# Lightning attention with a SwiGLU feed-forward block: the statements after the first chunks in a new, written-out order

## The chip, the cores and the metric

The kernel runs on one core of a Trainium2 chip. The metric is the device time of one execution in microseconds (us), as the median of several runs; less is better. The core has five engines that matter here, each with its own queue, which it works through in order: TensorE (PE in the profile; its weight loads are PEld), VectorE (DVE), ScalarE (ACT), GpSimd (POOL) and SyncE (SP), which only issues DMAs. They wait for each other through semaphores. Matmul results go to PSUM, which the kernel uses as eight banks of 128 partitions by 512 float32 columns.

## The reference

The input is q, k and v of shape 4 x 8 x 768 x 64 (batch, heads, positions, head size), a decay `lam` per head, and three weight matrices. The attention is linear, with a decay, in blocks of 64 positions:

```python
for b in range(nb):
    intra = einsum('bhic,bhjc->bhij', qb, kb) * Dmask      # inside the block
    intra = einsum('bhij,bhjd->bhid', intra, vb)
    inter = einsum('bhid,bhde->bhie', qb * lam_pow, kv_state)   # all earlier blocks
    out[:, :, sl] = intra + inter
    kv_state = lam_block * kv_state + einsum('bhsd,bhse->bhde', kb * rev_pow, vb)
```

Its result, as 3072 tokens of 512 values, goes through the feed-forward block, with 1536 hidden columns:

```python
g, val = x @ w_gate, x @ w_val
return (g * sigmoid(g) * val) @ w_out
```

## The kernel before, in words

**Attention.** The work is cut into 12 groups, numbered 0 to 11, of one pair of batches' 128 positions each (all eight heads). For each group the kernel loads q, k and v as float32, casts k and q to bf16 with the decay factors (`cast_scaled`: k on ScalarE, L291, q on VectorE or GpSimd, L293), transposes them by a DMA on SyncE's queue (L279), and scales v (`v_scale`, L266, mostly GpSimd). Then TensorE does four things in 64x64 tiles: `upd_mm` (L424, the sum of k times v that updates the state), `scores` (L362 or, from group 6 on, L392), `inter` (L518, queries times state) and `intra` (L531, masked scores times v). Most have 32 small matmuls. Around them, ScalarE copies the update out of PSUM (`upd_copy`, L438 and L446), GpSimd adds it to the running state (`state`, L459 to L483), VectorE multiplies the scores by the causal mask (L369, L397), and ScalarE's `guard` (L502) copies one column of the result between `inter` and `intra`, which share two banks, so that the second doesn't write into a bank while the first is still on its way. Last, `evac` (L544, L547) copies the result into `xt`, the input of the feed-forward block.

**Feed-forward.** Two groups make a tile of 512 tokens; there are six tiles, 0 to 5. In tiles 0 to 3 the hidden columns are taken in 12 chunks of 128: `ffn_gate` has four matmuls (L585), and ScalarE's silu of the result (L590); `ffn_val` has four (L603), and VectorE's multiplication with that silu (L607) gives the hidden values h. Tile 1 and the first chunks of tile 2 work on halves of 256 tokens, so there the matmuls have 256 columns instead of 512. Tile 0's output is a plain product (L623). Tiles 1 to 5 get their output by a Strassen-like scheme of seven products instead of eight (`out_units`, L823; p1 to p7), and tiles 4 and 5 use the same scheme for gate and value too (`ffn_unit`, L733, in three units per tile, with bank sums on VectorE at L775 and L783, copies on ScalarE at L767 and L770, and one of four multiplications on GpSimd, L763). The scheme needs sums of its operands: of the hidden values (`h_combo`, L670), of the weights (`w_combo`, L696, and `wo_combo`, L653) and of the inputs (`x_combo`, L714). All of these are on VectorE.

**What sets the order.** The first stretch, up to tile 0's chunk 1, is written out statement by statement. Behind it a plan decides: `steps` lists the feed-forward chunks, `at` hangs an attention part, a load or a sum behind a chunk, and a loop works through the chunks and hands out waiting work on the way: masks through `later`, sums through `trickle` (`drip` gives out one or two per chunk), state copies through `kvq`. Banks are taken in turn, 0 to 7 and around again, by `bank()`, where the plan doesn't set another start. From tile 2's output on, statements are written out, still with `drip` in between. A group's four TensorE parts stand mostly together, as in `attend`, called for groups 6 to 9:

```python
core_a(g)               # inter, guard
upd_mm(g + 1); upd_copy(g + 1)
scores(g + 1)
core_b(g)               # masks, intra, evac
state(g + 1)
```

Each engine runs its own instructions in the order in which the statements put them in its queue. Tile pools hand out buffers: four for the silu results, for instance, so that a chunk's silu waits until the multiplication four chunks earlier is done.

Of the kernel before, what the change touches and what calls it, by code (L numbers as in the profile page):

```python
# [37 lines left out]
def _body(ctx, tc, nc, q, k, v, lam, moe_w_gate, moe_w_val, moe_w_out, out):  # L38
# [13 lines left out]

    NAT0 = 6
    NB = 4
# [212 lines left out]
    def load_group(g, parts="kqv"):  # L271
        for src, what in ((k, "kraw"), (q, "qraw"), (v, "v")):
            if what[0] in parts:
                load_fp32(g, nc.scalar if what == "kraw" and g in KACT else nc.sync, src, what)

    def dma_transpose(g):
        t = st[("qk", g)]
        tt = qkt_pool.tile([128, 2, 2, HP, 128], BF16, name="qkt", tag="qkt")
        nc.sync.dma_start(out=tt.rearrange("p a s h n -> p (a s h) n"),  # L279
                          in_=t.rearrange("p a s x -> p (a s x)"), transpose=True)  # L280
        st[("qkt", g)] = tt
        for put in held.pop(g, []):
            put()

    QP = ()

    def cast_scaled(g, eng=nc.vector):
        eng = nc.gpsimd if g in QP else eng
        t = qk_pool.tile([128, 2, 2, H * D], BF16, name="qk", tag="qk")
        st[("qk", g)] = t  # L290
        nc.scalar.copy(out=t[:, 0].rearrange("p s (h d) -> p h s d", h=H),  # L291
                       in_=st[("kraw", g)].rearrange("p h (s d) -> p h s d", s=2))
        eng.tensor_tensor(out=t[:, 1].rearrange("p s (h d) -> p h s d", h=H),  # L293
                                in0=st[("qraw", g)].rearrange("p h (s d) -> p h s d", s=2),
                                in1=qfac(g), op=ALU.mult)
        dma_transpose(g)
# [38 lines left out]
    KACT = ()  # L335
    HOLD = {(1, 1): 10}
    held = {}
# [6 lines left out]
    def scores(g, cs=(0, 1), warm=0):  # L344
# [9 lines left out]
        for c in cs:  # L354
# [12 lines left out]
            for h2 in range(2):  # L367
                def do_mask(c=c, h2=h2):
                    nc.vector.tensor_tensor(  # L369
                        out=ssb[:, h2, 2 * c:2 * c + 2].rearrange("p a s n -> p a (s n)"),  # L370
                        in0=sp[(c, h2)].rearrange("p (a x) -> p a x", a=2),
                        in1=bap(causal, [[0, 2], [1, 2 * BLK]]),
                        op=ALU.mult)
                later.append(do_mask)
# [5 lines left out]
    def scores_n(g):  # L380
# [14 lines left out]
        for h2 in range(2):  # L395
            def do_mask(h2=h2):
                nc.vector.tensor_tensor(out=ssb[:, h2], in0=sp[h2].rearrange("p (a x) -> p a x", x=M),  # L397
                                        in1=bap(causaln, [[0, 2 * HP], [1, M]]), op=ALU.mult)
            later.append(do_mask)

    def upd(g):
        upd_mm(g)
        upd_copy(g)
        state(g)
# [58 lines left out]
    def kv_flush(age=0, m=9):  # L463
        while kvq and m and len(kvq_now) - kvq[0][0] >= age:
            kvq.pop(0)[1]()
            m -= 1

    def state(g):
# [5 lines left out]
        for n, u in enumerate(us):  # L474
# [9 lines left out]
            elif len(kv) == n + 1:  # L484
                o = kv_pool.tile([128, HP, D], BF16, name="kvn", tag=f"kvn{n}", bufs=2)
                kv.append(o)
                if g in KVA:
                    kvq.append((len(kvq_now), lambda g=g, n=n, o=o, f=f: kv_copy(g, n, o, f, nc.scalar.copy)))
                else:
                    kv_copy(g, n, o, f, nc.gpsimd.tensor_copy)  # L490


# [45 lines left out]
    def evac(g, fns=(nc.scalar.copy, nc.scalar.copy)):  # L538
        op, xt = st[("op", g)], st[("xt", g // 2)]
        for r in range(2):  # L540
            if fns[r] is None:
                continue
            if g < NAT0:
                fns[r](out=xt[:, g % 2, :, r].rearrange("p h (m s) -> p h s m", s=2),  # L544
                       in_=op[r].rearrange("p (h s m) -> p h s m", h=HP, s=2))
            else:
                fns[r](out=bap(xt, [[BLK, 2 * MC], [1, 2], [2, M // 2]], g % 2 * MC * 2 * BLK + r * M),  # L547
                       in_=op[r].rearrange("p (b e x) -> p b e x", b=2 * HP, e=2))
# [12 lines left out]

    def core(g, fns=(nc.scalar.copy, nc.scalar.copy)):
        core_a(g)
        core_b(g, fns)

# [65 lines left out]
    def take(n, seeded, cols):  # L631


        got = [(ring[0] + i) % 8 for i in range(n)]
        ring[0] += n
        yes = [x for x in got if primed[x] >= cols][:len(seeded)]
        assert len(yes) == len(seeded)
        rest = [x for x in got if x not in yes]
        return [yes.pop(0) if i in seeded else rest.pop(0) for i in range(n)]

# [14 lines left out]
    def h_combo(t, j, g=None):  # L655


        fs = slice(0, FH) if g is not None else slice(2 * j[0], 2 * j[1]) if type(j) is tuple else slice(2 * j, 2 * j + 2)
        g0, g1 = (0, B // 2) if g is None else (g, g + 1)
# [3 lines left out]
        for i in range(3):  # L663
            if ("hs", t, i) not in st:
                st[("hs", t, i)] = raw_pool.tile([128, FH, B // 2, BLK], BF16, name="hs", tag="raw")
# [624 lines left out]
```

## Time and profile before

| | |
|---|---|
| time, median of 3 runs | 217.0 us (216.41 to 217.78) |
| span of the profiled execution | 215.0 us (no other time of its own is given) |
| granted TensorE clock | 1.000 of full speed |
| TensorE matmul | 208.1 us busy, 97% |
| TensorE weight load | 153.3 us, 71% |
| VectorE | 148.3 us, 69% |
| ScalarE | 130.9 us, 61% |
| GpSimd | 92.7 us, 43% |
| moved by DMA | 39.76 MB |

The span goes from the first to the last instruction that the profiler records on the core. Busy time is the sum of an engine's instructions. A line of the timeline gives the start in us, the length in us, the engine, the program's line, the operation, out<-in by the program's names, and how many instructions are joined; what stands in brackets is the idle time ahead of it and what ended that. Matmuls overlap in their pipeline, so the length of a matmul line is longer than the time to the next one; distances between starts are the better measure. In a group line, the two numbers behind the bar are the busy time in us and the mean of one in ns; then follows the engine's idle time just before them and what ended it.

### The profile page before, as it was taken

The numbers are of one execution on the slowest core, as the hardware profiler recorded it, in microseconds if no ns is written. First come the engines' busy times: TensorE is split into PE (matmuls) and PEld (weight loads), VectorE is DVE, ScalarE is ACT, GpSimd is POOL, SyncE is SP. The second block draws the span as 40 slices with busy tenths as digits, with TensorE's granted clock in tenths as the row PEclk, the third lists the DMA queues.
The fourth block names the chain that finished last, engine by engine and source line by source line (L and its number), as shares of the span: only waits on it lengthen the run. The fifth ranks groups of instructions, "written<-read, shape, count | busy, mean of one in ns | idle before, by whom it ended". The sixth has DMA issues, their size and how long they took to land.

```text
span 215.0 us, 6856 instructions
## 1 busy us (share of the span) xinstructions
PE 208.1 (97%) x2797; PEld 153.3 (71%) x2801; DVE 148.3 (69%) x267; ACT 130.9 (61%) x280; POOL 92.7 (43%) x128
## 2 busy tenths in 40 slices
PE   8789999999999999999999999999999999999993
PEld 3467445887888548866754545888888888888883
DVE  1773447576677989874569878697988389961940
ACT  5878676756636153638369487774983676636522
POOL 6675755818399440595962153240750022200200
PEclk9999999999999999999999999999999999999999
DMA  6999999999999778899576859855000500005014
GB/s 188 345 354 381 376 336 296 285 226 223 309 387 174 185 212 208 244 214 263 122 198 143 217 121 257 207 121 201 5 3 5 195 0 3 0 0 198 0 52 146
DMA packets 82176, 39.76 MB, mean 185 GB/s; under 512 B 45410, under 2 KB 77794, under 8 KB 82146
## 3 DMA queue, kind: packets, MB, share of 16 engines
q1 hardware_dynamic: 80946, 38.74, 64.7%
q10 hardware_dynamic: 1200, 0.59, 0.9%
q8 instruction: 22, 0.36, 0.7%
q14 instruction: 8, 0.07, 0.1%
HBM read 28.31 MB, written 6.29 MB: 161 GB/s over the span
## 4 chain that ended last, share of the span: by engine, by line
PE 93%; DMA 2%; DVE 1%; SPq 1%; ACT 0%; issue 0%; DVEq 0%
PE bank L823 22%; PE bank L585 20%; PE bank L603 19%; PE bank L733 17%; PE bank L623 5%; PE bank L531 3%; DMA kraw<-in_k_dram 2%; PE bank L518 2%; PE bank L424 2%; PE bank L362 1%; DVE ssb L369 1%; SPq L115 1%; PE bank L392 1%; PE bank L322 1%; ACT qk L306 0%
## 5 line engine op out<-in xcount | busy, mean ns | idle before, releaser
L607 DVE TENSOR_TENSOR h<-sil,bank 128x256 bf16<-128x256 bf16 (+1 forms) x67 | 35.0, 533 | 29.9 <-PE bank L603 17.2
L585 PE MATMUL bank<-xt,wg_sb 128*128 128x256 bf16 (+1 forms) x276 | 52.8, 315 | 0.0
L603 PE MATMUL bank<-xt,wv_sb 128*128 128x256 bf16 (+1 forms) x276 | 52.5, 314 | 0.0
L590 ACT ACTIVATE sil<-bank 128x256 bf16<-128x256 f32 (+1 forms) x67 | 31.6, 481 | 21.8 <-PE bank L585 18.4
L603 PEld LDWEIGHTS <-wv_sb 128*128 128x128 bf16 x276 | 26.9, 98 | 14.8 <-POOL wv_sb L249 0.2
L585 PEld LDWEIGHTS <-wg_sb 128*128 128x128 bf16 x276 | 25.9, 98 | 13.6 <-issue 0.2
L266 POOL TENSOR_TENSOR v_s<-v,dec 128x512 bf16<-128x512 f32 (+1 forms) x18 | 23.0, 1295 | 24.3 <-DMA v<-in_v_dram 17.3
L763 POOL TENSOR_TENSOR h<-sil,es 128x512 bf16<-128x512 bf16 x6 | 7.0, 1165 | 47.4 <-ACT sil L760 47.4
L823 PEld LDWEIGHTS <-h 128*128 128x128 bf16 x240 | 23.3, 98 | 3.4 <-issue 0.3
L823 PE MATMUL bank<-wo_sb,h 128*128 128x256 bf16 x180 | 21.5, 273 | 0.0
L823 PEld LDWEIGHTS <-hs 128*128 128x128 bf16 x180 | 17.6, 98 | 2.7
L369 DVE TENSOR_TENSOR ssb<-bank,causal 128x512 bf16<-128x512 f32 x24 | 15.4, 684 | 1.8 <-PE bank L362 1.8
L479 POOL TENSOR_TENSOR kvf<-kvs,ups 128x256 f32<-128x256 f32 x8 | 6.5, 814 | 20.9 <-ACT ups L446 20.9
L733 PEld LDWEIGHTS <-ws 128*128 128x128 bf16 x144 | 13.8, 98 | 1.8
L823 PE MATMUL bank<-wt,hs 128*128 128x256 bf16 x120 | 15.0, 273 | 0.0
L775 DVE TENSOR_TENSOR bank<-bank,es 128x512 f32<-128x512 f32 x12 | 7.8, 694 | 9.6 <-PE bank L733 9.6
L479 POOL TENSOR_TENSOR kvf<-kvf,ups 128x256 f32<-128x256 f32 x16 | 13.0, 815 | 0.9
L760 ACT ACTIVATE sil<-bank 128x512 bf16<-128x512 f32 x18 | 10.5, 596 | 3.7 <-PE bank L733 3.7
L733 PE MATMUL bank<-xs,ws 128*128 128x256 bf16 x96 | 12.6, 273 | 0.0
L763 DVE TENSOR_TENSOR h<-sil,bank 128x512 bf16<-128x512 bf16 x18 | 11.8, 683 | 0.3 <-ACT sil L760 0.3
L623 PE MATMUL bank<-wo_sb,h 128*128 128x512 bf16 x45 | 10.7, 380 | 0.2
L733 PE MATMUL bank<-xt,wg_sb 128*128 128x256 bf16 x72 | 10.8, 273 | 0.0
(119 smaller groups left out, 360.3 us busy)
## 6 DMA issues: line engine op xcount, KB each, us to landing
out_dram<-osb SPq DMA_DIRECT2D x22, 256.0 KB, 2.6
v<-in_v_dram SPq DMA_DIRECT2D x18, 256.0 KB, 4.6
woraw<-in_moe_w_out_dram SPq DMA_DIRECT2D x6, 512.0 KB, 7.1
kraw<-in_k_dram SPq DMA_DIRECT2D x24, 128.0 KB, 3.4
qraw<-in_q_dram SPq DMA_DIRECT2D x24, 128.0 KB, 3.4
wraw<-in_moe_w_gate_dram SPq DMA_DIRECT2D x5, 512.0 KB, 6.9
wraw<-in_moe_w_val_dram SPq DMA_DIRECT2D x5, 512.0 KB, 7.0
kraw<-in_k_dram SPq DMA_DIRECT2D x4, 512.0 KB, 6.3
```

The source lines that it names most:

```text
L266: eng.tensor_tensor(out=st[("vs", g)][:, h0:h1], in0=st[("v", g)][:, h0:h1].rearrange("p h (s d) -> p h s d", s=2), in1=vfac(g, h0, h1), o ...
L369: nc.vector.tensor_tensor(out=ssb[:, h2, 2 * c:2 * c + 2].rearrange("p a s n -> p a (s n)"), in0=sp[(c, h2)].rearrange("p (a x) -> p a x", ...
L479: nc.gpsimd.tensor_tensor(out=o, in0=f, in1=u, op=ALU.add)
L585: nc.tensor.matmul(gp[:, n0:n1], wg_sb[:, mc, fs], xt[:, g0:g1, mc].rearrange("p g b n -> p g (b n)"), start=(mc == 0 and n0 == 0), stop=( ...
L590: nc.scalar.activation(sil[:, 0:N], gp[:, 0:N], AF.Silu)
L603: nc.tensor.matmul(vp[:, n0:n1], wv_sb[:, mc, fs], xt[:, g0:g1, mc].rearrange("p g b n -> p g (b n)"), start=(mc == 0 and n0 == 0), stop=( ...
L607: nc.vector.tensor_tensor(out=h_sb[:, fc % FH, b0:b1].rearrange("p b n -> p (b n)"), in0=sil[:, 0:N], in1=vp[:, 0:N], op=ALU.mult)
L623: nc.tensor.matmul(ps, st[("h", t, fc // FH)][:, fc % FH, b], wo_sb[:, fc, c0:c1], start=(fc == 0), stop=(fc == FC - 1))
L733: nc.tensor.matmul(o[:, fi * 256:fi * 256 + 256], lhs(i, c, 2 * j + fi), rhs(c), start=(start and fi == 0 and c == 0), stop=(c == KH - 1), ...
L760: nc.scalar.activation(sil[key], src, AF.Silu)
L763: eng.tensor_tensor(out=h_of(half, r), in0=v3(sil[half, r]), in1=v3(src), op=ALU.mult)
L823: nc.tensor.matmul(o, lhs(f), rhs(f), start=(start and f == 0), stop=(f == FH - 1), skip_group_check=True)
```

## The change

Everything up to tile 0's chunk 1 stays. From tile 0's third chunk on, the plan, the loop that works through it and the queues of waiting work are gone, and all statements are written out one by one, in another order. The functions are cut into smaller pieces for that: `core_a` and `core_b` become `op_new`, `inter`, `guard`, `intra` and `evr`; `cast_scaled` becomes `kcast` and `qcast`; `ffn_unit` becomes `unit`, `uprod` (one product with its copy or sum), `silu` and `mu`; `out_units` becomes `out_new`, `oprod` and `store`; `h_combo` becomes `hsum`, one sum each. `use(...)` names the banks for the statement behind it. `hsum`, `x_combo` and `w_combo` take the engine as an argument.

The computation, its tiles and its 2797 matmuls are the same. What moves: some chunks, or their value halves, now stand between the parts of a group's attention (groups 2, 3, 4 and 9, and group 10 in tile 4's second unit); gate and value chunks come in pairs in places; the q casts of groups 4 and 9, one weight sum (in three pieces), two input sums and seven sums of h go from VectorE to GpSimd; k cast 4 and some result copies go from ScalarE to VectorE; half the v scalings of groups 8 and 11 go from GpSimd to VectorE; the last output tile takes its products in another order.

```diff
-    def cast_scaled(g, eng=nc.vector):
-        eng = nc.gpsimd if g in QP else eng
...
+    def kcast(g, fn=nc.scalar.copy):
+        fn(out=qk_new(g)[:, 0].rearrange("p s (h d) -> p h s d", h=H),
+           in_=st[("kraw", g)].rearrange("p h (s d) -> p h s d", s=2))
+
+    def qcast(g, eng=nc.vector):
+        eng.tensor_tensor(out=qk_new(g)[:, 1].rearrange("p s (h d) -> p h s d", h=H),
...
+    def evr(g, r, fn):
         op, xt = st[("op", g)], st[("xt", g // 2)]
...
-    def core_a(g):
-        kv_flush()
+    def op_new(g):
         st[("op", g)] = [bank() for _ in range(2)]
         covered(2 * HP * D, 2)
-        inter(g, True)
-        guard(g)
-
-    def core_b(g, fns=(nc.scalar.copy, nc.scalar.copy)):
-        run_later(len(later))
-        intra(g, False)
-        evac(g, fns)
...
+    def hsum(t, k, f0, f1, g0=0, g1=2, eng=None):
+        fs = slice(f0, f1)
...
+        (eng or nc.vector).tensor_tensor(out=o, in0=i0, in1=i1, op=op)
+
+    def pair(o, i0, i1, op, eng=None, parts=1):
+        n = o.shape[-1] // parts if len(o.shape) == 3 else 0
...
-    at(s0["11a"], upd_core, 2, SPLIT)
-    at(s1a[7], scores, 3)
-    at(s1a[7], upd_mm, 3)
-    at(s1a[10], core_upd, 3, SPLIT, (0, 1))
-    at(s1b[9], core_upd, 4, SPLIT)
...
+    use(2, 3); upd_mm(2)
+    use(4, 5); op_bare(2)
+    intra(2, True)
+    guard(2)
+    upd_copy(2, (0,))
+    use(0); ffn_gate(0, 11, 0, 2)
+    inter(2, False)
+    evr(2, 0, DVEC)
+    evr(2, 1, ACTC)
...
+    kcast(4, DVEC)
+    use(3); ffn_val(1, 1, 0, 2)
+    state(2)
+    qcast(4, nc.gpsimd)
...
+    use(0, 4, 2, 3); scores(3)
+    use(6); ffn_gate(1, 8, 0, 2)
+    use(1, 5); upd_mm(3)
+    use(7); ffn_gate(1, 9, 0, 2)
+    upd_copy(3)
+    state(3)
+    use(6, 5); op_new(3)
...
+    use(3); ffn_val(1, 9, 0, 2)
+    use(7); ffn_val(1, 8, 0, 2)
+    mask(3, 1, 0)
+    inter(3, True)
+    guard(3)
+    use(3); ffn_gate(1, 10, 0, 2)
+    use(0, 1); upd_mm(4)
+    intra(3, False)
...
+    inter(4, True)
+    guard(4)
+    use(3); ffn_val(1, 9, 2, 4)
+    intra(4, False)
+    use(6, 7); upd_mm(5)
+    evr(4, 0, DVEC)
+    evr(4, 1, DVEC)
...
+    use(4, 5); op_new(7)
+    inter(7, True)
+    use(6, 7); upd_mm(8)
+    guard(7)
+    upd_copy(8)
+    intra(7, False)
+    use(0, 1); scores(8)
...
+    inter(9, True)
+    use(2, 3); upd_mm(10)
+    guard(9)
+    upd_copy(10)
+    use(4, 5); scores(10)
+    use(6); ffn_gate(3, 11, 0, 4)
+    intra(9, False)
+    evr(9, 0, ACTC)
+    evr(9, 1, ACTC)
+    hsum(2, 2, 4, 6, 0, 2, nc.gpsimd)
...
+    use(2, 4); upd_mm(11)
+    upd_copy(11)
+    state(11)
+    unit(4, 1, (3, 5, 2, 4, 6, 7))
+    uprod(4, 1, 0, 0)
+    uprod(4, 1, 0, 1)
+    intra(10, False)
...
+    mu(4, 1, 1, 1, nc.gpsimd)
+    uprod(4, 1, 5, 1)
+    uprod(4, 1, 5, 0)
```

More of the change, by code (lines that the diff above doesn't have):

```diff
@@ L395, in scores_n @@
         for h2 in range(2):
[L396 to L404, printed above, removed]
+            st[("sp", g, 0, h2)] = sp[h2]
+            later.append(lambda h2=h2: mask(g, 0, h2))
     def upd_mm(g, up=None):
@@ L755, in v3, with mu @@
+    def mu(t, j, half, r, eng=nc.vector):
         def v3(x):
             return x.rearrange("p (f g n) -> p f g n", f=2, g=2)
[L758 to L767 removed]
@@ new lines, in _body @@
+    use(7); ffn_val(2, 1, 0, 2)
+    use(0); ffn_gate(2, 2, 0, 2)
+    use(1); ffn_val(2, 2, 0, 2)
+    w_combo(1, 0, (0, 3), nc.gpsimd)
+    wo_combo(1)
+    use(2); ffn_gate(2, 3, 0, 2)
+    use(3); ffn_val(2, 3, 0, 2)
+    use(4); ffn_out(0, 0)
+    use(5, 1); op_new(5)
+    inter(5, True)
+    guard(5)
+    use(7, 0, 6, 2); scores(5)
+    mask(5, 0, 0)
+    mask(5, 1, 0)
+    mask(5, 0, 1)
+    mask(5, 1, 1)
+    use(3); ffn_out(0, 1)
+    intra(5, False)
+    kcast(6)
+    evr(5, 1, ACTC)
@@ new lines, in _body @@
+    use(5); ffn_val(3, 2, 0, 4)
+    use(3); ffn_val(3, 7, 0, 4)
+    hsum(2, 3, 0, 4, 0, 2)
+    hsum(2, 0, 4, 6, 0, 2)
+    use(6); ffn_gate(3, 3, 0, 4)
+    use(7); ffn_val(3, 3, 0, 4)
+    use(0, 1); op_new(8)
+    inter(8, True)
+    guard(8)
+    use(2, 3); upd_mm(9)
+    upd_copy(9)
+    use(4, 5); scores(9)
+    intra(8, False)
+    evr(8, 0, DVEC)
+    evr(8, 1, ACTC)
+    state(9)
+    use(6); ffn_gate(3, 8, 0, 4)
+    use(7); ffn_val(3, 8, 0, 4)
+    mask(9, 0, 1)
+    kcast(10)
+    qcast(10, nc.vector)
```

1144 lines of the change are left out of this document (709 added, 435 removed).

## The prediction

> **What bounds the kernel now.** I read the summary of the page first, then its chain, then TensorE's timeline from 15 us on.
>
> ```profile
> PE 208.1 (97%) x2797; PEld 153.3 (71%) x2801; DVE 148.3 (69%) x267; ACT 130.9 (61%) x280; POOL 92.7 (43%) x128
> ...
> PE 93%; DMA 2%; DVE 1%; SPq 1%; ACT 0%; issue 0%; DVEq 0%
> ...
> L763 POOL TENSOR_TENSOR h<-sil,es 128x512 bf16<-128x512 bf16 x6 | 7.0, 1165 | 47.4 <-ACT sil L760 47.4
> ```
>
> TensorE is busy 208.1 of 215.0 us and is 93% of the chain. Of its 6.9 us of idle time, 3.3 lie behind its last matmul (211.69, the last copies and stores, unchanged) and about 2.5 before 15 us (unchanged). So VectorE, ScalarE and GpSimd set the end only where a short wait of TensorE is theirs. The granted clock is 1.000 throughout, and the streaming rate doesn't move: a full-width matmul of 512 columns takes 0.216 us, one of 256 columns 0.109. The change keeps all 2797 matmuls with their shapes, so only two things can move the end: waits of TensorE, and what it loses between full-width work and the attention's 64x64 tiles (a **visit** below).
>
> Waits first, from TensorE's timeline:
>
> ```profile
> 37.51 0.45 PE L424 MATMUL bank<-v_s,qk 64*64 64x64 bf16 x32
> 37.79 0.67 PE L531 MATMUL bank<-ssb,v_s 64*64 64x128 bf16 x32
> 38.73 0.41 PE L518 MATMUL bank<-qkt,kvn 64*64 64x128 bf16 x8 [0.28 <-ACT guard L502]
> 39.07 0.39 PE L585 MATMUL bank<-xt,wg_sb 128*128 128x256 bf16 x2
> ...
> 52.80 0.59 PE L585 MATMUL bank<-xt,wg_sb 128*128 128x256 bf16 x2
> ...
> 99.55 1.03 PE L603 MATMUL bank<-xt,wv_sb 128*128 128x512 bf16 x4
> 100.59 0.38 PE L823 MATMUL bank<-wo_sb,h 128*128 128x256 bf16 x2
> ```
>
> Inside the visit at 37.51, TensorE stands 0.28 us for the guard copy. At 52.80 two matmuls take 0.59 where the same two take 0.39 at 39.07: 0.20 of waiting for the attention result's copy. From 99.55 to 100.59 four matmuls fill 1.04 where 4 x 0.216 = 0.86 would do: 0.18, waiting for a bank that two ScalarE copies empty. The visit at 132.09 lasts 1.40 where the same four parts at 108.79 and 122.17 last 1.18: 0.22. Together 0.88 us; what is left elsewhere after 20 us are gaps of 0.04 to 0.10, some 0.3 us. **So the waits that any new order could take away are about 1.2 us, under 1% of the time**, and 1% is about what a measurement of this kernel can tell from no change.
>
> Then the price of a visit. These are the shortest ones, with the full-width work around them:
>
> ```profile
> 145.71 0.60 PE L733 MATMUL bank<-xt,wv_sb 128*128 128x256 bf16 x4
> 146.24 0.45 PE L392 MATMUL bank<-qkt 64*64 64x64 bf16 x32
> 146.61 0.61 PE L733 MATMUL bank<-xs,ws 128*128 128x256 bf16 x4
> ...
> 86.28 0.60 PE L603 MATMUL bank<-xt,wv_sb 128*128 128x256 bf16 x4
> 86.81 0.45 PE L424 MATMUL bank<-v_s,qk 64*64 64x64 bf16 x32
> 87.08 0.46 PE L392 MATMUL bank<-qkt 64*64 64x64 bf16 x32
> 87.47 0.39 PE L823 MATMUL bank<-wo_sb,h 128*128 128x256 bf16 x2
> ```
>
> Four full-width matmuls from 145.71 stream until 145.71 + 4 x 0.109 = 146.15; the next full-width one starts at 146.61. The visit with one part of 32 matmuls costs 0.46 to 0.47. In the same way the one with two parts costs 87.47 - 86.28 - 0.437 = 0.75, and those with four 1.28 (0.10 before the first record, 1.18 after it). A line through 0.47, 0.75 and 1.28 has a slope of 0.27 per part and **0.20 per visit**: that is what TensorE loses in going to the small tiles and back.
>
> **The change, part by part.** *Visits.* Counted in the two programs, the redone part has 24 visits where before has 18. The six more: inter of group 2 is cut off from its upd and intra by half a gate chunk; scores and upd of group 3 are parted by a gate chunk; inter(3) from upd(4) and intra(3); inter(4) from intra(4) and upd(5), by a value half; intra(9) from inter(9), upd(10) and scores(10); upd(11) from intra(10), by two products. Cost: 6 x 0.20 = **+1.2 us**, on the path since TensorE has no slack. From below 6 x 0.13 = 0.8: 0.13 is 0.47 less a fourth of the visits that last longest (1.38 at 97.30, 0.345). Nothing here lets it be a gain.
>
> *Waits covered.* The guards of groups 2, 3, 4 and 9 now have full-width work, 0.43 to 0.86 us, between their inter and intra. All four waits above lie in orders that are gone: the result copies at 52.80 have more chunks behind them, and one of the two copies at 100 goes to VectorE. I take **-0.88** (between 0 and -1.2).
>
> *New waits.* The order before takes banks in turn, eight products apart; now each product names its bank and some come back fast. I went through all bank and buffer releases with row durations (silu of 256 columns 0.39, of 512 0.60; product copies 0.58; sums in a bank 0.69; a guard 0.16) and the latencies in the timeline (0.20 from a matmul group's end to ScalarE, 0.28 to VectorE, 0.05 back). Late are: value chunk (1,8) in bank 7, one chunk behind gate (1,9) in the same bank: 0.20 + 0.39 + 0.05 against 0.43 of work between, **0.21**. Guard(7), with only upd(8) between inter and intra since scores(8) moved behind: **0.16**. Product 5 of unit (4,1), whose bank sum is 0.14 late, and copies of group 10 in the same ScalarE queue, 0.1: **0.24**. The 0.09 for a sum of the output's products at 206 stays. Sum **+0.6** (0 to +1.2 as queue order may hide or double each). Behind each waiting matmul stands all of TensorE's queue.
>
> *Work moved to GpSimd.* GpSimd gains the q casts of groups 4 and 9 (row of one on GpSimd: 1.91), a weight sum in three pieces, two input sums and seven or so sums of h, and gives half a v scaling of groups 8 and 11 to VectorE. No GpSimd row shows a bf16 sum of two such buffers; the nearest, 128x512 L763, takes 1.165 against 0.42 to 0.44 on VectorE. GpSimd is 43% busy and idle for most of the time from 144 us on, so its own time hides: cost 0. The q cast of group 9 triggers its DMA transpose at about 116 as before (the SyncE queue's order is the same in both programs), landing 3.8 later, well before its scores. VectorE gains k cast 4 (1.05 on ScalarE before), two half scalings and result copies; it is 69% busy and those stand in its idle time.
>
> The bill of shared ports is the term no row settles for these places. VectorE's sum of 128x512 bf16 takes 0.42 at 140.90 and 1.20 at 142.32, where GpSimd scales v:
>
> ```profile
> 140.90 0.42 DVE L714 TENSOR_TENSOR xs<-xt,xs 128x512 bf16<-128x512 bf16 x1
> ...
> 142.32 1.20 DVE L714 TENSOR_TENSOR xs<-xt,xs 128x512 bf16<-128x512 bf16 x1
> ```
>
> and at 78.18 one of 128x768 takes 2.27 where its like take 0.56, beside a GpSimd scaling. So 0.78 to 1.71 per collision; in the forecast I let VectorE's slack (0.3 to 5 us at most places) swallow it: 0. *The Trainium skill, "SBUF — State Buffer", section "SBUF: two separate sides", says more: a VectorE instruction with two SBUF inputs and a GpSimd one lock each other out for a whole instruction. By that rule each moved sum can hold VectorE for its 1.165; with the three of the rival below that is 3.5 us in place of its 2.3. The trace has such holds, of 0.78 and 1.71; whether the short sums make them, no row here shows.*
>
> Sum: +1.2 - 0.88 + 0.6 = **+0.9**. The profiled span of 215.0 becomes 215.9; the profile gives no time of its own beside the span, and the median of the runs, 217.0, lies 2.0 above it (start and end, unchanged). Forecast **217.9 us**.
>
> **The rivals.** (1) *The new waits stay hidden*: some other engine runs ahead where I count it late. +1.2 - 0.88 = +0.3, and the gaps of 0.3 us may go too: 217.0 to 217.3. For it: most slacks are over 0.3 us. Against: the three spots are sums of measured durations.
>
> (2) *GpSimd holds VectorE; slower.* Place: 134 to 158, where GpSimd gets an input sum of tile 4, sums of h of tiles 3 and 4 beside its two h products and half a scaling, and VectorE is 82% busy (slices of 7 to 9 tenths). Three of the moved sums colliding at 0.78 give 2.3 us on VectorE's queue, behind which stand masks 11 and the bank sums of units (4,0) and (4,1), with slacks of 0.04 to 0.3. It decides as soon as a collision is longer than that slack: 217.9 + 2.3 = **220.2**. Against it: in before the row at 142.32 collided and TensorE stood nowhere near it.
>
> (3) *No wait is covered*, as the guard's and copies' waits only move to the next user of the same ScalarE queue (kvn of group 2 now stands behind guard(2)): 217.0 + 1.2 + 0.6 = **218.8**.
>
> (4) A gain over 1% would need 2.2 us, and waits hold 1.2: only if visits cost nothing.
>
> **Chances.** Forecast 0.52, (1) 0.15, (2) 0.20, (3) 0.09, (4) 0.04. Faster by over 1% 0.04; slower by over 1% (from 219.2) is (2) and the upper part of (3), 0.25; within 0.71. The range goes from (1) with all gaps covered and half a per cent of spread in the runs, 216.5, to (2), 220.3.
>
> **What would show it.** TensorE's timeline after: 24 visits, the new single ones 0.45 to 0.48 around full-width work; no wait for a guard in groups 2 to 4 and 9, one of about 0.16 at group 7; four value matmuls of (1,8) near 49 taking 0.21 longer than 0.43. Right for (2): VectorE sums over 1 us at 134 to 158 beside GpSimd's, and TensorE waiting for L775's successor. I am wrong if TensorE's idle plus visits in 20 to 212 grow by more than 2 us, or shrink.

## The result, and the profile after

The changed kernel takes 218.12 us (median of 13 runs, 216.64 to 219.76) against 217.02 of the kernel before (13 runs, 216.14 to 218.44). The ratio is 1.0062, with a 95% interval of 1.0042 to 1.0082: slower by 0.9 to 1.8 us, under 1%. The forecast was 217.9. The profiled execution of the changed kernel took 218.36 us with a span of 216.6: 1.8 us lie around the span here, and 1.7 to 1.8 in the later profiles.

The page of the changed kernel, summary, chain and the multiplications on GpSimd:

```profile
PE 208.6 (96%) x2797; PEld 152.8 (71%) x2801; DVE 148.9 (69%) x261; ACT 128.7 (59%) x276; POOL 110.3 (51%) x140
...
PE 82%; DMA 9%; POOL 3%; SPq 3%; issue 1%; ACT 1%; DVE 0%; DVEq 0%
...
L739 POOL TENSOR_TENSOR h<-sil,es 128x512 bf16<-128x512 bf16 x6 | 7.0, 1172 | 38.9 <-ACT sil L733 30.8
```

TensorE has the same 2797 matmuls in 208.6 us. GpSimd has 17.6 us more. The chain that ended last has only 82% of TensorE now, and 9% of DMA: somewhere it leaves TensorE and follows a load. TensorE's waits show where it could have left:

```profile
PE bank L182 <- PEq L1595: 0.8, 1, 0.8
PE bank L559 <- DVE h L581: 0.8, 1, 0.8
...
PE bank L408 <- POOL v_s L260: 0.2, 1, 0.2
```

The columns are the waiting group, what it waited for, the sum in us, how often, and the longest. The first is at the start of both kernels. The second and third are new. On TensorE's timeline (the rows at 36.46, 48.97 and 58.26 are of three different places):

```profile
36.46 0.25 PE L408 MATMUL bank<-v_s,qk 64*64 64x64 bf16 x8
36.90 0.38 PE L408 MATMUL bank<-v_s,qk 64*64 64x64 bf16 x24 [0.18 <-POOL v_s L260]
37.09 0.64 PE L513 MATMUL bank<-ssb,v_s 64*64 64x128 bf16 x32
37.66 0.61 PE L559 MATMUL bank<-xt,wg_sb 128*128 128x256 bf16 x4
38.29 0.41 PE L500 MATMUL bank<-qkt,kvn 64*64 64x128 bf16 x8
38.63 0.61 PE L559 MATMUL bank<-xt,wg_sb 128*128 128x256 bf16 x4
...
48.97 1.23 PE L577 MATMUL bank<-xt,wv_sb 128*128 128x256 bf16 x8
50.42 0.41 PE L500 MATMUL bank<-qkt,kvn 64*64 64x128 bf16 x8 [0.22 <-ACT ups L430]
...
58.26 0.60 PE L577 MATMUL bank<-xt,wv_sb 128*128 128x256 bf16 x4
59.66 0.60 PE L559 MATMUL bank<-xt,wg_sb 128*128 128x256 bf16 x4 [0.80 <-DVE h L581]
```

The half gate chunk at 37.66 now stands between intra and inter of group 2, and the wait for the guard that was there before is nearly gone. The upd at 36.46 stops after 8 of 32 matmuls, for the second half of the scaled v. The eight value matmuls at 48.97 take 1.23 where two groups of four usually take 1.04: 0.20 for the short bank turn-around of chunk (1,8). And from 58.26 to 59.66 four matmuls of 0.109 each fill 1.40 us: a wait of 0.96, which the forecast doesn't have.

**A ledger of TensorE.** From 19.2 us on I add up, in one profiled execution of each kernel, what lies between full-width matmuls beyond their streaming time (0.2157, 0.1092 or 0.056 us by width): visits to the 64x64 tiles with their length, and gaps. Three gaps of 0.216 in the first output are left out in each kernel; they have the length of one matmul whose record is missing.

| us | before | changed | difference |
|---|---|---|---|
| start of the last matmul | 211.40 | 212.84 | +1.44 |
| visits, number | 18 | 24 | +6 |
| visits, sum of lengths | 17.52 | 18.38 | +0.86 |
| gaps, sum | 1.13 | 1.71 | +0.58 |
| of these, the gap at 58.69 | - | 0.96 | +0.96 |

Outside the two waits that are looked at next (0.96 at 58.69, and 0.37 in the visit at 36.4), the changed order costs TensorE only 0.1 us more than the one before. Experiment 8 has a second execution of each.

### The profile page after: what moved, and what is told of

Read it like the earlier page. It is cut to its first block, busy times and chain, and to the rows that moved or that the text cites. A ratio compares the mean times of both kernels' runs of the same rounds, so it can differ in the third digit from the quotient of the medians.

```text
span 216.6 us, 6848 instructions
## 1 busy us (share of the span) xinstructions
PE 208.6 (96%) x2797; PEld 152.8 (71%) x2801; DVE 148.9 (69%) x261; ACT 128.7 (59%) x276; POOL 110.3 (51%) x140
## 4 chain that ended last, share of the span: by engine, by line
PE 82%; DMA 9%; POOL 3%; SPq 3%; issue 1%; ACT 1%; DVE 0%; DVEq 0%
PE bank L773 21%; PE bank L714 17%; PE bank L559 16%; PE bank L577 15%; DMA wraw<-in_moe_w_val_dram 7%; PE bank L597 5%; SPq L109 3%; PE bank L513 2%; DMA v<-in_v_dram 2%; PE bank L500 2%; POOL v_s L260 2%; PE bank L408 2%; POOL wv_sb L243 1%; PE bank L383 1%; PE bank L347 1%
## 5 line engine op out<-in xcount | busy, mean ns | idle before, releaser
L559 PE MATMUL bank<-xt,wg_sb 128*128 128x256 bf16 (+1 forms) x276 | 50.9, 315 | 0.8 <-DVE h L581 0.8
L577 PE MATMUL bank<-xt,wv_sb 128*128 128x256 bf16 (+1 forms) x276 | 50.5, 315 | 0.0
L260 POOL TENSOR_TENSOR v_s<-v,dec 128x512 bf16<-128x512 f32 (+1 forms) x16 | 21.4, 1351 | 8.8 <-DMA v<-in_v_dram 8.8
L462 POOL TENSOR_TENSOR kvf<-kvs,ups 128x256 f32<-128x256 f32 x8 | 6.0, 750 | 27.4 <-ACT ups L430 27.4
L773 PEld LDWEIGHTS <-hs 128*128 128x128 bf16 x180 | 17.6, 98 | 2.9
L462 POOL TENSOR_TENSOR kvf<-kvf,ups 128x256 f32<-128x256 f32 x16 | 13.9, 868 | 0.9
```

The lines of the kernel that those rows point to most:

```text
L260: eng.tensor_tensor(out=st[("vs", g)][:, h0:h1], in0=st[("v", g)][:, h0:h1].rearrange("p h (s d) -> p h s d", s=2), in1=vfac(g, h0, h1), o ...
L462: nc.gpsimd.tensor_tensor(out=o, in0=f, in1=u, op=ALU.add)
L559: nc.tensor.matmul(gp[:, n0:n1], wg_sb[:, mc, fs], xt[:, g0:g1, mc].rearrange("p g b n -> p g (b n)"), start=(mc == 0 and n0 == 0), stop=( ...
L577: nc.tensor.matmul(vp[:, n0:n1], wv_sb[:, mc, fs], xt[:, g0:g1, mc].rearrange("p g b n -> p g (b n)"), start=(mc == 0 and n0 == 0), stop=( ...
L773: nc.tensor.matmul(o, lhs(f), rhs(f), start=(k in (1, 7) and f == 0), stop=(f == FH - 1), skip_group_check=True)
```

## Experiments

Each kernel was timed beside the kernel before on the same chip. "Last matmul" is its start in the profiled execution (211.40 before, 212.84 changed).

### 1. The wait at 58.69: one scaling moved

```diff
     use(0); ffn_val(1, 4, 2, 4)
-    v_scale(5, nc.gpsimd)
     use(3); ffn_val(1, 3, 2, 4)
...
     wo_cast()
+    v_scale(5, nc.gpsimd)
     wo_cast()
```

> The changed kernel with one move: the v scaling of group 5 stands again behind the first weight cast on GpSimd's queue instead of ahead of all five. Theory H (held VectorE): in the changed kernel this scaling (56.28 to 58.19) runs beside VectorE's q cast of group 5, which takes 2.59 us instead of 1.22 to 1.30; the h products behind it come late and TensorE waits 0.96 us for a silu buffer at 58.69. With the scaling behind a weight cast, the q cast takes 1.2 to 1.3 and the wait is gone: the last matmul starts 0.9 to 1.0 us earlier (about 211.9 instead of 212.84), 217.2 us. Theory Q (the queue's order): VectorE has the q cast ahead of the h products in either case, and the wait comes from that; then 0.9 stays and nothing moves.

Measured: 217.37 us (12 runs), ratio 1.0040 (1.0024 to 1.0056); last matmul 211.87, 0.97 earlier; no gap at 58.7. VectorE and GpSimd in the changed kernel:

```profile
56.68 2.59 DVE L282 TENSOR_TENSOR qk<-qraw,dec 128x1024 bf16<-128x1024 f32 x1
59.20 1.07 DVE L581 TENSOR_TENSOR h<-sil,bank 128x256 bf16<-128x256 bf16 x3
...
56.28 1.91 POOL L260 TENSOR_TENSOR v_s<-v,dec 128x1024 bf16<-128x1024 f32 x1
```

and with the scaling moved:

```profile
56.68 1.22 DVE L282 TENSOR_TENSOR qk<-qraw,dec 128x1024 bf16<-128x1024 f32 x1
57.82 0.74 DVE L581 TENSOR_TENSOR h<-sil,bank 128x256 bf16<-128x256 bf16 x2
...
58.65 1.04 POOL L254 CAST wo_sb<-woraw 128x1024 bf16<-128x1024 f32 x1 [2.32 <-DMA woraw<-in_moe_w_out_dram]
59.66 1.92 POOL L260 TENSOR_TENSOR v_s<-v,dec 128x1024 bf16<-128x1024 f32 x1
```

The q cast starts at 56.68 in both. Beside the scaling, which had started 0.40 earlier and ended at 58.19, it lasts 2.59; alone, 1.22. Three h products queue behind it, a silu waits for their buffer, and TensorE for that silu's bank. In the first profile of the kernel before the two do not meet:

```profile
56.23 1.22 DVE L293 TENSOR_TENSOR qk<-qraw,dec 128x1024 bf16<-128x1024 f32 x1
...
60.61 1.91 POOL L266 TENSOR_TENSOR v_s<-v,dec 128x1024 bf16<-128x1024 f32 x1
```

Theory H holds for this wait, theory Q (the queue's order) doesn't. The ratio falls by 0.2%, less than the 0.45% of this one execution, and the two intervals (1.0042 to 1.0082, 1.0024 to 1.0056) overlap: the trace shows the wait and its cause, the times do not show how much of the slowdown is this wait's. See experiment 8.

### 2. The same collision in the kernel before

```diff
+    at(s1b[2], v_scale, 5, nc.gpsimd)
     at(s1b[2], cast_scaled, 5)
...
-    at(s1b[4], v_scale, 5, nc.gpsimd)
```

> The kernel before with the v scaling of group 5 put ahead of its q cast in the plan, so that both run at once. Theory H: the q cast on VectorE goes from about 1.2 to over 2 us, and TensorE gets a wait of 0.5 to 1.0 us near 57 to 60 that the kernel before doesn't have; last matmul about 212.0 to 212.4 instead of 211.40. Theory Q: no new wait, since the plan hands out chunks in the same order as before.

Measured: 216.78 us (one run, before 216.44 on that chip), last matmul 211.52. The expected wait did not come. VectorE and GpSimd:

```profile
55.95 1.22 DVE L293 TENSOR_TENSOR qk<-qraw,dec 128x1024 bf16<-128x1024 f32 x1
...
56.66 2.28 POOL L266 TENSOR_TENSOR v_s<-v,dec 128x1024 bf16<-128x1024 f32 x1 [0.70 <-DMA v<-in_v_dram]
```

The load of v landed at 56.66, after the q cast had started. Now the cast has its usual 1.22 and the scaling is longer, 2.28 instead of 1.91. So it isn't the meeting that decides but who is first. Collected over all runs with the two close together:

| run | scaling starts | q cast starts | q cast takes | scaling takes | wait of TensorE |
|---|---|---|---|---|---|
| changed | 56.28 | 56.68 | 2.59 | 1.91 | 0.96 |
| experiment 3 (sums on VectorE) | 55.90 | 56.30 | 2.60 | 1.92 | 0.97 |
| experiment 7 (guards rejoined) | 56.45 | 56.61 | 2.83 | 1.91 | 1.20 |
| experiment 4 (six more visits) | 57.10 | 57.13 | 2.97 | 1.91 | 1.34 |
| experiment 5 (two rejoined) | 56.48 | 56.42 | 1.22 | 2.93 | 0 |
| experiment 2 (this one) | 56.66 | 55.95 | 1.22 | 2.28 | 0 |
| experiment 6 (other banks) | 57.62 | 56.79 | 1.22 | 2.15 | 0 |
| changed, once more | 58.25 | 56.33 | 1.22 | 1.91 | 0 |

The first keeps its time, the second gets the rest of the first on top: with 1.88 us of scaling left (experiment 4) the cast is 1.75 longer, with 1.51 left (changed) 1.37, each 0.13 to 0.14 less than the rest. In the last row the cast is done before the scaling starts, and both have their usual length. The Trainium skill, "SBUF — State Buffer", section "SBUF: two separate sides", states this as an exclusive lock that the one who starts first holds for its whole instruction; the seven rows in which the two meet agree with it.

### 3. The sums that the change gave GpSimd

```diff
-    w_combo(1, 0, (0, 3), nc.gpsimd)
+    w_combo(1, 0, (0, 3))
...
-    hsum(2, 2, 4, 6, 0, 2, nc.gpsimd)
+    hsum(2, 2, 4, 6, 0, 2)
...
-    x_combo(4, 1, None, nc.gpsimd)
+    x_combo(4, 1, None)
...
```

and so for all ten.

> The changed kernel with all ten sums that it gives GpSimd (one weight sum, two input sums, seven sums of h) back on VectorE, in the same places; the two q casts and the scalings stay. If the moved sums hold VectorE at a price (rival 2 of the prediction), TensorE gains here, up to 2.3 us. If VectorE's slack swallows the collisions, as forecast, nothing moves (within 0.3 us), or it is a little slower, since VectorE's queue is longer by about 10 sums of 0.42 to 1.2 us, 5 to 6 us in all.

Measured: 218.88 us (4 runs), ratio 1.0105 (1.0072 to 1.0138); last matmul 213.95, 1.1 later than in the changed kernel. So taking these sums off GpSimd wins nothing; with them on VectorE, in these places, the kernel isn't faster, and by the middle of the two ratios 0.4% slower (the intervals still overlap). TensorE's new gaps in this kernel are 0.79 at 104.84, 0.28 at 186 (in two pieces), and 0.41 at 207.43 that the changed kernel doesn't have; the first comes with a late load of q (group 8), as VectorE's own rows show:

```profile
103.15 1.23 DVE L282 TENSOR_TENSOR qk<-qraw,qdn 128x1024 bf16<-128x1024 f32 x1 [1.66 <-DMA qraw<-in_q_dram]
104.29 0.68 DVE L581 TENSOR_TENSOR h<-sil,bank 128x512 bf16<-128x512 bf16 x1
104.89 0.68 DVE L358 TENSOR_TENSOR ssb<-bank,causaln 128x512 bf16<-128x512 f32 x1
```

The 0.28 and 0.41 are late in the kernel, where nothing is loaded; the 0.41 ended with a sum of h on VectorE, and the 0.28 is most likely the sums' too. Collisions are there in the changed kernel: at 138.68 a sum on VectorE takes 1.38 instead of 0.42 beside one on GpSimd. TensorE has no gap near it.

```profile
138.68 1.38 DVE L632 TENSOR_TENSOR hs<-h,hs 128x512 bf16<-128x512 bf16 x1
139.98 0.42 DVE L782 TENSOR_TENSOR bank<-bank,osb 128x256 f32<-128x256 f32 x1
...
138.44 1.33 POOL L678 TENSOR_TENSOR xs<-xt,xs 128x512 bf16<-128x512 bf16 x1 [1.40 <-DVE xs L678]
```

### 4. The price of a visit: six more

```diff
     use(0, 1); upd_mm(4)
+    use(7); ffn_val(1, 10, 0, 2)
     intra(3, False)
...
-    use(7); ffn_val(1, 10, 0, 2)
...
-    use(7); ffn_val(2, 4, 0, 4)
     use(0, 1); upd_mm(6)
...
+    use(7); ffn_val(2, 4, 0, 4)
     use(2, 3); scores(6)
```

and four more like these.

> The changed kernel with six further visits cut in two by a chunk that stood beside them (groups 4 with 3, 5 with 4, 6, 7 with 6, 9 with 8, 10 with 9): 30 visits instead of 24, and nothing else. By the forecast a visit costs TensorE 0.20 us in going to the 64x64 tiles and back: +1.2 us, last matmul at about 214.0. A rival: the loss at the edges overlaps with the streaming on both sides, and a visit costs half of that or less: +0.6 or below. Waits for guards that the cuts cover may give 0.1 to 0.3 back (groups 7 with 6 and 9 with 8).

Measured: 220.17 us (4 runs), ratio 1.0149 (1.0110 to 1.0187), that is 1.9 us over the changed kernel's ratio; last matmul 215.05, 2.2 later. In the ledger the visits sum to 19.16 instead of 18.38. The changed kernel's 18.38 has the 0.37 of waiting for the scaled v at 36.4, which isn't in this execution: six visits cost 19.16 - 18.01 = 1.15, **0.19 each** in the mean (0.18 to 0.22 at five places, 0.12 at the one, groups 7 and 6, where the uncut visit holds some waiting). One of them, upd and scores of group 6, which were one visit of 0.76:

```profile
87.81 0.60 PE L577 MATMUL bank<-xt,wv_sb 128*128 128x256 bf16 x4
88.34 0.45 PE L408 MATMUL bank<-v_s,qk 64*64 64x64 bf16 x32
88.72 1.05 PE L577 MATMUL bank<-xt,wv_sb 128*128 128x256 bf16 x8
89.69 0.45 PE L383 MATMUL bank<-qkt 64*64 64x64 bf16 x32
90.07 0.61 PE L773 MATMUL bank<-wo_sb,h 128*128 128x256 bf16 x4
```

From the end of the four at 87.81 (88.25) to 88.72 is 0.47, and from 88.72 + 8 x 0.109 = 89.60 to 90.07 is 0.47 again: 0.94 for what took 0.76. The rival (half of it) falls. The rest of the 2.2 us isn't the visits': the gap at 59 grew from 0.96 to 1.34, a new one of 0.41 stands at 102, the 0.37 went, and 0.5 lies before the redone part (the first visit starts at 33.63 instead of 33.09).

### 5. Two cuts that seemed to hide nothing

```diff
-    use(0, 4, 2, 3); scores(3)
     use(6); ffn_gate(1, 8, 0, 2)
+    use(0, 4, 2, 3); scores(3)
...
     use(2, 4); upd_mm(11)
+    intra(10, False)
...
-    intra(10, False)
```

> The changed kernel with two visits put together again: gate chunk (1,8) ahead of scores(3) instead of behind it, and intra(10) directly behind upd(11). Neither cut hides a wait by the trace. 22 visits: 0.4 us less (2 x 0.20), last matmul at about 212.4, unless the masks of group 3 or ScalarE's copies come later for it and give back 0.1 to 0.3.

Measured: 217.96 us (one run); last matmul 212.52, 0.3 earlier. upd(11) and intra(10) together last 0.72 instead of 0.465 + 0.471: 0.22 won. scores(3) and upd(3) together last 0.92 instead of 0.667 + 0.471: 0.22 won as well. The value chunks behind them wait 0.17 and 0.04, the first for a bank that a mask of group 3 still reads; but the 0.20 for which the changed kernel waits at the second one (the short turn-around of bank 7) has shrunk to that 0.04, so the waits there sum to 0.20 in both kernels. By the trace the two joins win 0.43, as expected, and with these banks neither of the two cuts hides anything. (With other banks the cut of group 3 does: experiment 9.) The last matmul shows only 0.3 of it: the wait at 58.69 is gone in this execution (the q cast started 0.06 ahead of the scaling), and one of 1.14 at 104 has come, where VectorE waited 1.98 for q of group 8.

### 6. Other banks around group 3

```diff
-    use(6, 5); op_new(3)
+    use(6, 4); op_new(3)
...
-    use(7); ffn_val(1, 8, 0, 2)
+    use(0); ffn_val(1, 8, 0, 2)
...
-    use(4); ffn_gate(1, 0, 2, 4)
+    use(5); ffn_gate(1, 0, 2, 4)
...
-    use(5); ffn_val(1, 0, 2, 4)
+    use(4); ffn_val(1, 0, 2, 4)
```

> The changed kernel with other banks around group 3: value chunk (1,8) in bank 0 instead of bank 7, the result of group 3 in banks 6 and 4 instead of 6 and 5 (and gate and value of (1,0), second half, in 5 and 4 instead of 4 and 5). Theory of short bank turn-arounds: the gap of 0.20 at 49.41 goes, and the visit of inter(3) at 50.04, which lasts 0.73 where inter(2) with as many matmuls lasts 0.53, falls to 0.45 to 0.5: TensorE's last matmul 0.4 to 0.5 earlier, about 212.4. Rival: inter(3) waits for the state copy that ScalarE makes just before, and not for the bank; then only the 0.20 goes.

Measured: 217.41 us (one run); last matmul 211.98. The gap of 0.20 at 49.4 is gone, and the visit of inter(3) lasts 0.436 instead of 0.727: both were short bank turn-arounds, 0.49 in all, and the rival (a state copy) falls: the changed kernel's state copy was done at 49.82, 0.6 ahead of inter(3). The collision of group 5 costs TensorE nothing in this execution (the q cast came first), but the next visit lasts 2.00 instead of 0.92, for v of group 4, whose load landed at 49.45 (47.93 in the changed kernel's profile):

```profile
49.79 0.61 PE L559 MATMUL bank<-xt,wg_sb 128*128 128x256 bf16 x4
51.41 0.45 PE L408 MATMUL bank<-v_s,qk 64*64 64x64 bf16 x32 [1.01 <-POOL v_s L260]
51.67 0.64 PE L513 MATMUL bank<-ssb,v_s 64*64 64x128 bf16 x32
...
49.45 1.91 POOL L260 TENSOR_TENSOR v_s<-v,dec 128x1024 bf16<-128x1024 f32 x1 [3.05 <-DMA v<-in_v_dram]
```

### 7. The cuts behind the guards taken back

```diff
+    use(0); ffn_gate(0, 11, 0, 2)
     use(2, 3); upd_mm(2)
...
-    use(0); ffn_gate(0, 11, 0, 2)
     inter(2, False)
```

and in the same way for groups 3, 4 and 9.

> The changed kernel with the four cuts taken back that stand behind a guard (groups 2, 3, 4 and 9): the chunk or half chunk goes ahead of the visit. 20 visits. By the ledger of the two traces a cut pays by the wait that it hides, less 0.20: group 2 0.2, group 3 0, group 4 0.07, group 9 0.05. So this kernel is 0.3 us slower than the changed one (last matmul about 213.1). Rival: the cuts pay nothing or cost, since the visits are what counts: 0.8 us faster less small waits, about 212.3.

Measured: 217.40 us (9 runs, 217.31 to 219.50), ratio 1.0049 (1.0019 to 1.0079), which overlaps with the changed kernel's interval; last matmul 213.17, 0.33 later, of which 0.24 are the wait of group 5 (1.20 instead of 0.96). By the two traces the cuts of groups 2 and 4 pay (group 2: 1.90 in one visit against 0.92 + 0.53 in two, without the 0.37 for the scaled v; group 4: 1.81 against 0.66 + 0.92), the one of group 9 is even (1.42 against 0.98 + 0.47), and the one of group 3 costs (1.33, and 0.11 in a gap, against 0.73 + 0.92). Together the four are worth 0.4 us there, near the 0.3 that was expected. The times lean the other way (1.0049 against 1.0062) and do not separate the two, so what the cuts behind guards are worth on average stays open.

### 8. The changed kernel and the kernel before, once more

> The changed kernel once more, unchanged, to see which of its waits are in every execution. By structure: 24 visits, gaps of 0.20 at 49.4 and 0.14 at 157.6, the visit of 1.45 at 110. By the order of starts, which loads decide: the q cast of group 5 at 2.5 to 3 us with a wait of 0.9 to 1.3 us if the scaling of v(5) starts first (its load landed early), and 1.22 without a wait if it starts second; the wait for the scaled v of group 2 near 36.5 (0.37) may be there or not.

Measured: 216.95 us (one run), last matmul 211.52, 1.3 us earlier than in the first profile of the same program. The gaps at 49 (0.20) and 156 (0.135) and the visit at 108 (1.45) are there again, as expected. The wait for group 5 isn't, nor the one at 36.5:

```profile
56.33 1.22 DVE L282 TENSOR_TENSOR qk<-qraw,dec 128x1024 bf16<-128x1024 f32 x1
...
58.25 1.91 POOL L260 TENSOR_TENSOR v_s<-v,dec 128x1024 bf16<-128x1024 f32 x1 [2.29 <-DMA v<-in_v_dram]
```

This time the load of v(5) landed at 58.25, where the first profile had the scaling start at 56.28, and that was better: the scaling came after the q cast.

The wait at 36.5 comes from a load too, by way of GpSimd's queue. In the first profile the cast of a value weight starts when its load lands, and the scalings of v of group 2 stand behind it:

```profile
33.79 1.04 POOL L243 CAST wv_sb<-wraw 128x1024 bf16<-128x1024 f32 x1 [2.09 <-DMA wraw<-in_moe_w_val_dram]
34.79 2.05 POOL L260 TENSOR_TENSOR v_s<-v,dec 128x512 bf16<-128x512 f32 x2
```

In the second profile that cast starts at 33.06 and the scalings at 34.34, 0.45 earlier, and TensorE doesn't wait. The chain of the first profile goes through this load (27.45 to 33.73) and these two rows.

> The kernel before once more, unchanged, as a second look at its own scatter. By structure: 18 visits with the same lengths, the guard waits in the visits at 37 and 62, gaps of 0.21 at 52.9, 0.18 at 100.4, 0.10 at 184.7 and 207.5. If loads decide part of its time too, one more wait of TensorE of 0.3 us or more shows up somewhere before 105 us, or one goes; if the kernel before has slack for its loads where the changed one hasn't, the ledger is the same within 0.2 us (last matmul 211.2 to 211.6).

Measured: 217.21 us (one run), last matmul 211.96. All visits up to 63 are equal within 0.02; then a gap of 0.54 at 68.4 that the first profile doesn't have, 0.22 more in the visit at 72, 0.23 more at 52.6, and 0.16 less in the visit at 132: 0.8 us of waits more, of which the start, 0.3 us earlier, takes some back. The largest comes from a load: ScalarE waited 1.90 us for output weights and gave out five silus late.

```profile
68.93 0.60 PE L585 MATMUL bank<-xt,wg_sb 128*128 128x256 bf16 x4 [0.38 <-ACT sil L590]
...
67.55 1.04 ACT L260 CAST wo_sb<-woraw 128x1024 bf16<-128x1024 f32 x1 [1.90 <-DMA woraw<-in_moe_w_out_dram]
68.50 1.47 ACT L590 ACTIVATE sil<-bank 128x256 bf16<-128x256 f32 x5
```

So the kernel before has waits that come and go too: 0.8 us between its two profiles, 1.3 between those of the changed one. In these second profiles the changed kernel's last matmul is 0.44 *earlier* than that of the kernel before (211.52 against 211.96), and its visits and gaps sum to 0.7 us less, where the first pair has 1.44 more. That the changed kernel is slower is shown by the 13 timed runs of each, not by one pair of traces. Its 13 runs go from 216.64 to 219.76, so the second profile (216.95) is one of its shortest executions.

### 9. All repairs together

The moves of 1, 5 and 6, and:

```diff
+    use(6); ffn_gate(0, 11, 2, 4)
     use(2, 3); upd_mm(2)
...
-    use(6); ffn_gate(0, 11, 2, 4)
     use(1); ffn_val(0, 11, 0, 2)
...
-    intra(7, False)
     use(0, 1); scores(8)
+    intra(7, False)
...
     uprod(4, 1, 3, 1)
+    uprod(4, 1, 5, 0)
     uprod(4, 1, 4, 1)
...
-    uprod(4, 1, 5, 0)
     silu(4, 1, 1, 0)
```

> The changed kernel with everything that the traces point to: v scaling of group 5 behind a weight cast (1.0), other banks around group 3 (0.4 to 0.5), half a gate chunk of (0,11) ahead of upd(2) so that its scaled v is ready (0.0 to 0.4), scores(8) ahead of intra(7) again so that its guard is covered (0.17), the two visits put together (0.4), and product 5 of tile 4's second unit, gate side, ahead of product 4's value side, so that a bank sum is not waited for (0.14). Sum 2.1 to 2.6: last matmul at 210.3 to 210.8 against 211.40 of the kernel before and 212.84 of the changed one; 216.2 us, 0.3 to 0.5% faster than the kernel before. Rival: each repaired wait uncovers the next one, as TensorE only catches up with the engines that feed it; then it stays at the time of the kernel before or above.

Measured: 217.07 us (12 runs), ratio 1.0003 (0.9979 to 1.0028); last matmul 212.25. Each repaired place is repaired (the visit of group 7 is 1.28 instead of 1.45, no gap at 157), the two value chunks at 48.7 and 49.3 wait 0.16 each for masks, and one gap of 1.15 at 53.31 is new. The trace names nothing that this gate matmul waited for ("issue"), and I can't say what it was:

```profile
53.20 0.27 PE L559 MATMUL bank<-xt,wg_sb 128*128 128x256 bf16 x1
54.45 0.93 PE L559 MATMUL bank<-xt,wg_sb 128*128 128x256 bf16 x7 [0.98 <-issue]
```

It stands behind the first of a chunk's four matmuls, which all write the same bank, so it isn't a wait for a bank. As the intervals of this kernel (0.9979 to 1.0028) and of the changed one (1.0042 to 1.0082) are apart, the repairs together take the slowdown away; the gain of 0.3 to 0.5% over the kernel before did not come.

Against that kernel, the cut of group 3 set again:

```diff
-    use(6); ffn_gate(1, 8, 0, 2)
     use(0, 4, 2, 3); scores(3)
+    use(6); ffn_gate(1, 8, 0, 2)
     use(1, 5); upd_mm(3)
```

> The kernel with all repairs, but with the cut between scores(3) and upd(3) kept (gate chunk (1,8) behind scores(3), as in the changed kernel). In the two kernels where those were put together, the value chunks at 48.7 and 49.3 each waited 0.16 us for a bank that a mask still reads: the cut hides the masks of group 3. So putting them together won 0.25 and lost 0.33 or more. Expected here: 23 visits, no gaps at 48.7 and 49.3, last matmul at 210.8 to 211.2 if no load lands late, 0.2 to 0.3% faster than the kernel before. Rival: TensorE, now earlier, waits for loads (v of group 4, q of group 8 land within 1 us of need), and gives it back: equal to the kernel before.

Measured: 217.20 us (12 runs, 216.04 to 218.87), ratio 1.0022 (0.9995 to 1.0049). The profiled execution is the best of all: 216.11 us, last matmul 210.59, gaps of 0.2 us in all. But only 5 of the 12 runs lie near it (216.04 to 216.59); seven are at 217.16 to 218.87. Between 46 and 52 us the visits and gaps sum to 0.26 less than in the kernel with the two joined: with the short turn-arounds gone, this cut pays, by hiding the masks. In the profiled execution TensorE ends 0.8 us ahead of the kernel before; most executions give it back. That late loads do it, as the rival has it, fits experiments 5 and 6, but isn't shown for these runs, which have no profile.

And on top of it one load moved:

```diff
+    load_fp32(4, nc.sync, v, "v")
     dma_transpose(3)
-    load_fp32(4, nc.sync, v, "v")
```

> The same, and the load of v of group 4 is issued on SyncE's queue ahead of the transpose of group 3 instead of behind it (issue near 38.2 instead of 43.4). In the runs so far the scaling of v(4) began at 47.7 to 49.5, whenever the load landed, and in one of them upd(4) waited 1.0 us for it. If late loads take the gain away, this one shows v(4) scaled at least 1 us earlier, no wait at 50 to 52, and a time below that of the kernel without the move by up to 0.5 us on average. If loads aren't the cause, no change.

Measured: 217.38 us (12 runs), ratio 1.0038 (1.0018 to 1.0057): no gain. v(4) is scaled at 46.46 as expected, 1.9 us earlier, but the transpose of group 3 comes later for it, and its scores wait:

```profile
45.90 1.04 PE L577 MATMUL bank<-xt,wv_sb 128*128 128x256 bf16 x8
48.25 0.64 PE L347 MATMUL bank<-qkt 64*64 64x128 bf16 x32 [1.32 <-DMA qkt<-qk]
```

Its transpose took 4.81 us from its issue instead of 2.45. What the one load gained in this execution, the next transfer lost.

## Why the prediction was right, and where it wasn't

The time (217.9 forecast, 218.12 measured; +0.9 forecast, +0.9 to +1.8 measured) and the sign are right. That the number is so near is in part luck: the terms behind it were wrong by more than 1 us in both directions, and the 2.0 us that the prediction adds for what lies around the span are 1.7 to 1.8 in every later profile. The terms, by the ledger of the two profiled executions:

| term | forecast | measured | shown by |
|---|---|---|---|
| six more visits | +1.2 | +1.15 | experiment 4: 0.19 each, on six others |
| waits covered | -0.88 | -2.0 | ledger |
| new waits of the written order | +0.6 | +0.9 | ledger, experiment 6 |
| VectorE held by GpSimd | 0 | +0.96, not in each execution | experiments 1, 2, 8 |
| late scaled v of group 2 (a weight load) | none | +0.37, not in each execution | experiment 8 |
| sum | +0.9 | +1.4 | last matmul +1.44 |

*Visits.* The 0.20 per visit, read from the line through visits of one, two and four parts, was right; six further visits showed it (0.19). The Trainium skill, "TensorEngine Tiling (Array Packing)", section "Key Properties", says that a change of tiling mode drains TensorE. The runs agree that the change costs time: the 0.19 is its price for the way there and back.

*Waits covered: mis-sized, by 1.1 us.* I took the guard wait of group 2 from the bracket in the timeline, 0.28. The bracket counts from the modelled end of the last matmul, which lies behind the end of its streaming (the prediction's row at 145.71 is 0.60 long for 0.44 of streaming), so it shows a wait too short, here by 0.2. By parts (0.20 for the visit, 0.72 for upd and intra, 0.24 for the eight inter matmuls, from visits without a wait) the visit of 1.65 holds 0.49 of waiting. In the same way group 4's visit at 62.4 held 0.27, which I did not count at all, and the one at 50.5 held 0.21. With the 0.22 at 132.0 that is 1.2 in visits, and 0.8 in gaps, also the 0.17 around the transposes at 31, which come and go with the execution.

*New waits.* The three that I found by walking the banks were there with the right size: chunk (1,8) 0.20 (forecast 0.21), guard(7) 0.17 (0.16), the bank sum of unit (4,1) 0.135 (0.14). The 0.1 for group 10's copies did not come. Missed: inter(3), 0.29, whose second bank is the one that upd(3) just had (experiment 6), and 0.09 at inter(2).

*VectorE held by GpSimd: the step that failed.* I let VectorE's slack swallow all collisions and put the price of rival 2 on the moved sums, at 134 to 158. The runs showed the mechanism of that rival, but not its cause or its place: taking the moved sums back makes nothing faster (experiment 3), and the one at 138.68 collides for 0.96 us and no matmul waits. What costs 0.96 us in this execution is the scaling of v(5), which the new order puts ahead of the weight casts and so beside a q cast at 56 us, with three h products behind it and no slack. The prediction doesn't mention this move at all: it priced what the change gives to GpSimd, and not what only changes its place in GpSimd's queue.

*The other rivals.* That the new waits would stay hidden (1) is wrong, they were there. That no wait is covered (3) is wrong; more was covered than I counted. A gain over 1% (4) did not come, though the 1.2 us of waits on which its refusal rests were at least 2.0.

So two errors, 1.1 too little gain and 1.3 too little loss, nearly cancel. By the ledger, visits, covered waits and the new waits that are in both executions sum to about +0.1 us: the order by itself costs TensorE next to nothing, and nearly all of the +1.4 in the first profile are waits that come and go. How often each of them comes in the timed runs isn't shown. So the causes of these two waits are shown, but how the 0.9 to 1.8 us of the timed runs divide among them stays open; experiment 9 shows only that repairs worth 2.1 to 2.6 us by the ledger take the slowdown away. What happens in the first 60 us, where loads land, decides about as much as the order: the same program gave a last matmul at 212.84 and at 211.52. The prediction's own sign of being wrong, that TensorE's idle time and visits shrink, would have come from the second pair of profiles and did not come from the first.

## What to carry to other kernels

Price each move of an instruction by what then runs beside it on an engine that can hold it up (here GpSimd and VectorE), not only by the queue it stands in: a 1.9 us operation set next to a 1.2 us one cost 1 us of TensorE, in some executions and not in others. A cut between small-tile parts costs about 0.2 us here, so it must hide more than that, and masks, guards and bank releases behind it are part of the count. In an order without slack, measure more than one profile before you explain a difference of one per cent: here two executions of the same program differed by as much as the whole change.

## What the runs showed of the hardware that I had not expected

- An earlier load cost TensorE time. With v(5) there by 56.28 the scaling ran ahead of the q cast (which took 2.59 us, and TensorE waited 0.96); with v(5) landing at 58.25 it came behind, and nothing waited.
- Whoever of VectorE and GpSimd starts first keeps its own time, even by 0.03 us (57.10 against 57.13: the cast takes 2.97); the other pays nearly the whole rest. With the cast first by 0.06 us the scaling takes 2.93 instead of 1.91.
- A sum on GpSimd can lengthen one on VectorE from 0.42 to 1.38 (138.68), and still taking the ten moved sums back into VectorE's own queue made the kernel no faster (experiment 3).
